# An attention and MLP kernel on one core: a tile's softmax kept in its scores' PSUM bank, the low half of g in the next slot, global results turned on TensorE

## The chip, the cores and the metric

One core of a Trainium2 chip. The metric is device microseconds (us) of one execution, lower is better. The profile is one execution, taken by the hardware profiler. Engines: PE is TensorE's matmul and PEld its weight load, DVE is VectorE, ACT is ScalarE, POOL is GpSimd, and SP is the engine whose queue issues the DMAs here. SBUF is the working memory, PSUM the banks into which PE writes.

## The reference

Eight batches with eight heads of attention over 512 local and 32 global positions, then a two-layer product over all 4608 tokens. A local query sees the 32 global keys and the local keys within 32 positions; a global query sees all keys.

```python
k_all = np.concatenate([k_g, k_l], axis=2); v_all = np.concatenate([v_g, v_l], axis=2)
out_g = np.matmul(sm(scale * np.matmul(q_g, k_all.transpose(0, 1, 3, 2))), v_all)
s_ll = np.where(np.abs(pos[:, None] - pos[None, :]) <= 32, scale * np.matmul(q_l, k_l.transpose(0, 1, 3, 2)), -1e9)
out_l = np.matmul(sm(np.concatenate([s_lg, s_ll], axis=-1)), np.concatenate([v_g, v_l], axis=2))
x = np.concatenate([out_g, out_l], axis=2).transpose(0, 2, 1, 3).reshape(4608, 512)
h = np.maximum(x @ w_in, 0.0)          # 512 -> 2048
return h * h @ w_out                   # 2048 -> 512
```

`sm` subtracts the row's maximum, takes the exponential and divides by the sum plus 1e-9.

## The kernel before, in words

**Tiles.** An attention tile t is one head of one half sequence: 256 queries (two groups u of 128), each group against 224 keys, out of 128 tiles. The first 16 tiles ("plain") are computed in float32, all others with operands split into a high and a low float32r half (`hi`/`lo`, `ph`/`pl`, `gh`/`gl`, `x_h`/`x_l`, `ws`): three products in place of one. The MLP runs in 17 blocks of 256 tokens, of eight steps m each; a step forms 256 of the 2048 hidden columns (`gemm1`, tile h), squares the positive part (`act1`), splits it (`act2`) and adds its share of the output (`gemm2`, tiles o).

**The slot.** One turn of the main loop holds tile t and step m = t - 9. The instructions of each engine are issued in the order in which the code names them (`InOrder`, from t = 17 on), so the code's order is each engine's queue. Within a slot, for tile t: `scores` (PE, tile s), `softmax1` (DVE: mask, scale, row minimum), `softmax2` (ACT: exponential with sums), `softmax3` (DVE: 1e-9 added to the sums, tile st, reciprocal, normalisation into prob), `turn` (POOL copies prob's 16-bit words into planes, then a transposing DMA into turned). For tile t - 1: `join` (POOL, turned to joined), `parts` (ACT, ph) and `parts_rest` (DVE, ph, ml, pl), and late in the slot `av` (PE, tile xa). For t - 2: `x_evac` (ACT x_h, DVE x_l). For t + 1: `split_qk` (ACT) and `split_qk_rest` (DVE), tile qk, from raw. For t + 2: `load_head`, the DMA of raw, into one of two buffers. `split_v` makes the two halves of tile t's v out of raw (ACT, DVE).

**PE's order** in a slot is h (24 matmuls), gs, half of o, now and then a global product gxo, the other half of o, xa of tile t - 1, s of tile t + 1. The scores of a tile lie in one PSUM bank (pool `ps_a`, tag "s"), which the next tile's scores take again.

**Global jobs.** Each group of four heads with its 32 global queries needs some fifteen jobs (`g_load_v`, `g_soft`, `g_turn`, `g_join`, `g_parts`, `g_av`, `g_x` and so on). The dictionary `jobs` sets each at a slot, relative to d, and at a place in the slot. Two such groups fall into 16 slots. `g_av` writes its result gxo into the bank of xa, ACT scales it into xs, and `g_x` turns it by four DVE transposes of 32x32 into xg.

**Shared ports.** DVE and POOL both work on SBUF: POOL's copies are joined, planes, and for the global jobs gp<-sg (`g_turn`) and sg<-gq (`g_join`).

Of the kernel before, what the change touches and what calls it, by code (L numbers as in the profile page):

```python
# [17 lines left out]
P = 128  # L18
# [41 lines left out]
def attention_moe(  # L60
# [88 lines left out]
    def split_v(t):  # L149
        raw = heads[t]["raw"]  # L150
        v = heads[t]["v"] = p2.tile([P, 2, 192], F32R, tag="v", name=f"v{t}")
        ac.copy(v[:, 0, :], raw[:, QK:])
        ve.tensor_sub(v[:, 1, :], raw[:, QK:], f(v[:, 0, :]))

    def scores(t):
        hd = heads[t]
        pool, tag = (ps_h, "h") if t < 8 and t % 2 else (ps_a, "s")
        s = pool.tile([P, 2, WIN], F32, tag=tag, name=f"s{t}")
# [12 lines left out]

    def softmax1(t):
        hd = heads[t]
        hf = (t // 8) % 2
        pr = p2.tile([P, QK + QC], F32, tag="qk", name=f"pr{t}")[:, : 2 * WIN] if plain(t) else prob
        hd["pr"] = pr
        st = p2.tile([P, 8], F32, tag="st", name=f"st{t}")
        for u in range(2):
            m = 2 * hf + u
            ve.tensor_tensor_reduce(  # L180
                out=pr[:, WIN * u : WIN * (u + 1)],
                in0=hd["s"][:, u, :],
                in1=masks[:, WIN * m : WIN * (m + 1)],
                scale=-scale(t),
                scalar=3.0e38,
                op0=ALU.add,
                op1=ALU.min,
                accum_out=st[:, u : u + 1],
            )
        hd["st"] = st  # L190

    def softmax2(t):
        st = heads[t]["st"]
        pr = heads[t]["pr"]
        for u in range(2):
            w_ = pr[:, WIN * u : WIN * (u + 1)]
            ac.activation(
                out=w_, in_=w_, func=AF.Exp, scale=-1.0, bias=st[:, u : u + 1], accum_out=st[:, 4 + u : 5 + u]
            )

    def softmax3(t):
# [41 lines left out]
    def parts_rest(t):  # L243
# [4 lines left out]
        ve.tensor_sub(pl.rearrange("p (c n) -> p c n", c=2), sides(joined), sides(f(ph)))  # L248

    def av(t):  # L250
        hd = heads[t]
        c = QC + KC
        if plain(t):

            xa = ps_a.tile([P, HALF], F32, tag="xa", name=f"xa{t}")
            v, pts = hd["raw"][:, c:], hd["pts"]
# [5 lines left out]
        else:  # L262
            xa = ps_a.tile([64, HALF], F32, tag="xa", name=f"xa{t}")
            v, ph, pl = hd["v"], hd["ph"], hd["pl"]
# [13 lines left out]
    def x_evac(t):  # L278
# [123 lines left out]
    def g_av(t, pair):  # L402
        (gvh, gvl), (pth, ptl) = state["gvs"], state["gpt"]
        xo = ps_a.tile([64, P], F32, tag="xa", name=f"gxo{t}_{pair}")
        mm = []
# [4 lines left out]
        for i, (x, y) in enumerate(mm):  # L410
            pe.matmul(xo, x, y, start=i == 0, stop=i == len(mm) - 1)
        xs = p1.tile([64, P], F32, tag="xs", name=f"gxs{t}_{pair}")
        ac.activation(out=xs, in_=xo, func=AF.Copy, scale=state["gst", t][:64, pair : pair + 1])
        state["xs"] = xs

    def g_x(t, pair):
        b, grp, xs = t // 16, (t // 4) % 2, state["xs"]
        for j in range(2):
            h = 4 * grp + 2 * pair + j
            for dd in range(2):  # L420
                r = (h % 2) * 64 + 32 * dd
# [73 lines left out]
    def act2(m):  # L495
# [118 lines left out]
    for t in range(NSTEP + LAG + 1):  # L614
# [40 lines left out]
        for place in (4, 3):
            for job, *args in jobs.pop((t, place), ()):
                job(*args)
        if done:
            evac(m // 8 - 1, (1,))
# [154 lines left out]
```

## Time and profile before

| | |
|---|---|
| median of three runs | 1070.45 us (1070.18 to 1073.39) |
| the profiled execution | 1071.19 us, of which the span of the program's instructions 1069.1 |
| busy: PE, PEld | 1029.5 (96%), 902.3 (84%) |
| busy: DVE, ACT, POOL | 867.7 (81%), 721.5 (67%), 385.0 (36%) |
| chain that ended last | PE 43%, DVE 37%, ACT 8%, issue 5%, DMA 3%, POOL 2% |
| granted PE clock, mean | 0.994 |

The span falls into a start in float32 that is bound by loads and PE (to about 106 us), five slots in which the last weights are split (to 154 us), the steady part (to 961 us) and an end in which only the MLP is left. Matmuls are pipelined, so PE's busy time is a union of overlapping intervals. A row of a group of instructions ends in its busy time, the mean of one in ns, and the engine's idle time just before them; a row by tile gives minimum/median/maximum in ns. DVE instructions that are held up show as long instructions, not as idle time.

### The profile page before, as it was taken

To read this page: it belongs to the slowest core of one execution; us is meant where nothing else is said; L and a number is where in the kernel's file an instruction comes from. 1 tells how busy PE (TensorE), PEld (TensorE's weight loads), DVE (VectorE), ACT (ScalarE), POOL (GpSimd) and SP (SyncE) were. 2 spreads that over 40 slices of the span, in tenths; PEclk is the share of its full clock that TensorE was granted. 3 is DMA by queue.
4 is the path that set the end of the run, shared out by engine and by line. 5 is a ranking of instruction groups with operands and counts; after the bars stand their busy time and mean duration, and the time that the engine had idled before them with its cause. 6 is when DMAs were issued, how large, how long until landed. Compare 5 with 4: busy or idle time off the path is not lost.

```text
span 1069.1 us, 20564 instructions
## 1 busy us (share of the span) xinstructions
PE 1029.5 (96%) x7040; PEld 902.3 (84%) x7040; DVE 867.7 (81%) x2445; ACT 721.5 (67%) x1743; POOL 385.0 (36%) x544
## 2 busy tenths in 40 slices
PE   8999989999999999999999999999999999999998
PEld 6776778988898888888888889888888888889896
DVE  5689878899989888898979999898989999893311
ACT  6889766767767766767666766776667676664432
POOL 1010344444445343444444443453445353441000
PEclk9999989999999999999999999999999999999999
DMA  9772444445444544454544444545444454341000
GB/s 367 310 258 80 104 103 115 114 116 125 116 123 101 136 103 101 115 118 123 122 115 116 116 120 109 123 104 125 125 110 105 118 135 110 103 95 54 5 21 20
DMA packets 193576, 127.69 MB, mean 119 GB/s; under 512 B 143552, under 2 KB 168640, under 8 KB 193472
## 3 DMA queue, kind: packets, MB, share of 16 engines
q1 hardware_dynamic: 193328, 126.32, 44.5%
q8 instruction: 55, 0.90, 0.4%
q14 instruction: 49, 0.40, 0.1%
q10 hardware_dynamic: 144, 0.07, 0.0%
HBM read 82.84 MB, written 8.91 MB: 86 GB/s over the span
## 4 chain that ended last, share of the span: by engine, by line
PE 43%; DVE 37%; ACT 8%; issue 5%; DMA 3%; POOL 2%; SPq 0%; DVEq 0%; POOLq 0%; ACTq 0%
PE o L53 17%; PE h L53 16%; DVE prob L53 6%; DVE st L53 5%; DVE qk L53 5%; PE xa L53 4%; ACT prob L53 3%; DVE v L53 3%; PE s L53 3%; DVE gl L53 2%; PE gxo L53 2%; DVE x_l L53 2%; DVE ph L53 2%; DVE pl L53 2%; DMA raw<-in_pk_dram 2%
## 5 line engine op out<-in xcount | busy, mean ns | idle before, releaser
L53 PE MATMUL h<-x_h,ws 128*128 128x256 f32 x2048 | 391.4, 284 | 0.0
L53 PEld LDWEIGHTS h<-x_h,ws 128*128 128x128 f32 x2048 | 329.1, 192 | 0.7
L53 PE MATMUL o<-ws,gh 128*128 128x512 f32 x1024 | 324.4, 398 | 3.2 <-ACT ot L53 3.0
L53 PE MATMUL h<-x_l,ws 128*128 128x256 f32 x1024 | 290.9, 284 | 1.1 <-DVE x_l L53 1.1
L53 POOL COPY joined<-turned 128x1024 uint16<-128x1024 uint16 x112 | 155.3, 1387 | 378.1 <-DMA turned<-planes 232.9
L53 POOL COPY planes<-prob 128x448 uint16<-128x448 uint16 x336 | 171.3, 547 | 152.1 <-DVE prob L53 152.1
L53 PEld LDWEIGHTS o<-ws,gh 128*128 128x128 f32 x1024 | 182.5, 189 | 38.2 <-ACT ot L53 7.0
L53 PE MATMUL o<-ws,gl 128*128 128x512 f32 x512 | 202.1, 395 | 0.0
L53 PEld LDWEIGHTS h<-x_l,ws 128*128 128x128 f32 x1024 | 197.0, 192 | 3.2 <-DVE x_l L53 2.6
L53 ACT ACTIVATE prob<-prob,st 128x224 f32<-128x224 f32 x224 | 106.3, 475 | 90.3 <-DVE st L53 89.5
L53 DVE TENSOR_TENSOR gl<-pt,gh 128x512 fp32r<-128x512 f32 x128 | 87.5, 684 | 73.2 <-ACT gh L53 72.0
L53 DVE TENSOR_TENSOR qk<-raw,qk 64x352 fp32r<-64x352 f32 x224 | 109.1, 487 | 8.7 <-ACT qk L53 1.6
L53 PEld LDWEIGHTS o<-ws,gl 128*128 128x128 f32 x512 | 96.3, 188 | 23.1
L53 ACT ACTIVATE pt<-h 128x512 f32<-128x512 f32 x128 | 74.2, 580 | 54.3 <-PE h L53 54.0
L53 ACT CAST x_h<-xa 64x256 fp32r<-64x256 f32 x120 | 43.7, 364 | 98.2 <-PE xa L53 97.9
L53 ACT CAST ph<-joined 128x512 fp32r<-128x512 f32 x112 | 68.9, 615 | 41.2 <-POOL joined L53 39.0
L53 PE MATMUL s<-qk 128*128 128x224 f32 x448 | 83.5, 298 | 8.2 <-DVE qk L53 5.6
L53 DVE TENSOR_SCALAR st<-st 128x2 f32<-128x2 f32 x128 | 62.5, 488 | 34.0 <-ACT prob L53 29.8
L53 ACT CAST qk<-raw 128x608 fp32r<-128x608 f32 x112 | 78.1, 697 | 8.7 <-DMA raw<-in_pk_dram 8.6
L53 DVE TENSOR_TENSOR v<-raw,v 128x192 fp32r<-128x192 f32 x112 | 80.5, 719 | 0.0
L53 DVE CUSTOM_DVE_ANT_0 prob<-s,con 128x224 f32<-128x224 f32 x224 | 77.7, 382 | 3.0 <-PE s L53 1.3
L53 ACT ACTIVATE pt<-pt 128x512 f32<-128x512 f32 x128 | 74.5, 582 | 4.0
(85 smaller groups left out, 1616.9 us busy)
## 6 DMA issues: line engine op xcount, KB each, us to landing
raw<-in_pk_dram SPq DMA_DIRECT2D x112, 400.0 KB, 3.5
wr<-in_w_dram SPq DMA_DIRECT2D x32, 512.0 KB, 8.0
gv<-in_vg_dram SPq DMA_DIRECT2D x32, 320.0 KB, 3.8
out_dram<-ot SPq DMA_DIRECT2D x32, 256.0 KB, 2.4
raw<-in_pk_dram SPq DMA_DIRECT2D x15, 432.0 KB, 8.2
qr<-in_qg_dram SPq DMA_DIRECT2D x31, 64.0 KB, 3.1
turned<-planes SPq DMA_TRANSPOSE x112, 3.1
out_dram<-ot SPq DMA_DIRECT2D x8, 64.0 KB, 1.7
```

Source lines behind the costliest of these rows:

```text
L53: r = method(*args, **kwargs)
```

## The change

For tiles from 16 on, `softmax1` writes its masked scores back into the scores' bank and `softmax2` takes the exponential in place there; the normalisation reads the bank and writes prob to SBUF. The sums go into two columns of the PSUM tile of xa (that of tile t - 2, read out by then), and st reads them there. The low half gl of step m - 1 is computed in slot m (`act2_rest`), behind `softmax1`. `split_qk`, its rest, `parts` and its rest follow the normalisation, in this order, and the low half of v comes last (up to tile 21 it stays early). Both output evictions stand ahead of the exponential, and their tiles take the buffers of gl and gh instead of two of the global jobs'. The global jobs are at other slots and places; gxo lies in the scores' bank, and the turning of the result is one PE transpose into 64 free columns of that bank and two ACT copies, in place of four DVE transposes.

```diff
+    def work(t, u):
+        hd = heads[t]
+        return hd["pr"][:, WIN * u : WIN * (u + 1)] if plain(t) else hd["s"][:, u, :]
     def softmax1(t):
...
-                out=pr[:, WIN * u : WIN * (u + 1)],
+                out=work(t, u),
     def softmax2(t):
+        su = st[:, 4:6] if plain(t) else state["xa"][:, HALF:]
...
-                out=w_, in_=w_, func=AF.Exp, scale=-1.0, bias=st[:, u : u + 1], accum_out=st[:, 4 + u : 5 + u]
+                out=w_, in_=w_, func=AF.Exp, scale=-1.0, bias=st[:, u : u + 1], accum_out=su[:, u : u + 1]
     def softmax3(t):
-        ve.tensor_scalar(out=st[:, 6:8], in0=st[:, 4:6], scalar1=1e-9, scalar2=None, op0=ALU.add)
+        ve.tensor_scalar(out=st[:, 6:8], in0=heads[t]["sums"], scalar1=1e-9, scalar2=None, op0=ALU.add)
...
-                ve.tensor_scalar(out=w_, in0=w_, scalar1=st[:, 2 + u : 3 + u], scalar2=None, op0=ALU.mult)
+                ve.tensor_scalar(out=to, in0=work(t, u), scalar1=by, scalar2=None, op0=ALU.mult)
+    def out_bank(t):
+        state["xa"] = ps_a.tile([P, HALF + 2], F32, tag="xa", name=f"xa{t}")
+        return state["xa"]
     def g_av(t, pair):
-        xo = ps_a.tile([64, P], F32, tag="xa", name=f"gxo{t}_{pair}")
+        xo = ps_a.tile([P, 512], F32, tag="s", name=f"gxo{t}_{pair}")[:64, :P]
     def g_x(t, pair):
-                ve.transpose(
+        xt = state["s"][:, 2 * WIN :]
+        pe.transpose(xt, state["xs"], ident[:64, :64])
+    def g_x_copy(t, pair):
+            ac.copy(xg[r, 2 * grp + pair, 32 * b : 32 * b + 32], xt[r, 32 * j : 32 * j + 32])
     def act2(m):
-        ve.tensor_sub(gl, r, f(gh))
+    def act2_rest(m):
+        ve.tensor_sub(gl, moe["r"], f(gh))
     def evac(blk, tiles=(0, 1)):
-            pool, tag = ((p1, "ptl"), (p1, "gvl"))[i]
+            pool, tag = ((p2, "gl"), (p2, "gh"))[i]
```

In the main loop the calls of a slot are put in another order (a job's second number is its place in the slot):

```diff
         if live:
             softmax1(t)
+        if 8 < m <= NSTEP:
+            act2_rest(m - 1)
...
         if live and not early:
             split_v(t)
+            if t < LATE:
+                split_v_rest(t)
+        for job, *args in jobs.pop((t, 7), ()):
...
         if live:
             softmax2(t)
-        if new:
-            parts(t - 1)
+        for job, *args in jobs.pop((t, 4), ()):
...
         if live and not early:
             softmax3(t)
             turn(t)
+        for job, *args in jobs.pop((t, 9), ()):
...
+        if t + 1 < NT and not early:
+            split_qk(t + 1)
+        if new:
+            parts(t - 1)
+        if not early:
+            if t + 1 < NT:
+                split_qk_rest(t + 1)
+            if new:
+                parts_rest(t - 1)
+            if live and t >= LATE:
+                split_v_rest(t)
         if NPLAIN <= t + 2 < NT:
             load_head(t + 2)
```

And the jobs of a global group, each with its slot and place:

```diff
+            first = t % 8 == 3
+            k = d + 7 if first else d + 6
-                (d + 4, 3, g_parts),
-                (d + 4, 0, g_av, 0),
-                (max(d + 5, 17), 3, g_x, 0),
-                (d + 5, 2, g_split_v, 1),
-                (max(d + 6, 17), 0, g_av, 1),
-                (max(d + 7, 18), 3, g_x, 1),
+                ((d + 5, 9, g_parts) if first else (d + 4, 3, g_parts)),
+                (d + 5, 0, g_av, 0),
+                (d + 5, 0, g_xs, 0),
+                (d + 6, 7, g_x, 0),
+                (d + 6, 4, g_x_copy, 0),
+                ((d + 6, 3, g_split_v, 1) if first else (d + 5, 1, g_split_v, 1)),
+                (k, 0, g_av, 1),
+                (k, 0, g_xs, 1),
+                (k + 1, 7, g_x, 1),
+                (k + 1, 4, g_x_copy, 1),
```

DVE's queue in slot 78, before the change, from the second masked reduction on (the number behind a tile's name is the attention tile or the step: gl69 belongs to step 69):

```order
L53 TENSOR_TENSOR v78_7375<-raw78_7191,v78_7375 128x192
L53 TENSOR_SCALAR st78_7359<-st78_7359 128x2
L53 RECIPROCAL st78_7359<-st78_7359 128x2
L53 TENSOR_SCALAR prob_93<-prob_93,st78_7359 128x224 x2
L53 TENSOR_TENSOR gvl75_0_7393<-gv75_0_7124,gvh75_0_7392 128x512
L53 TENSOR_TENSOR gvh75_0_7392<-gv75_0_7124,gvh75_0_7392 32x128
L53 TENSOR_TENSOR ph77_7380<-joined_96,ph77_7380 32x256
L53 TENSOR_TENSOR ml_97<-joined_96,ph77_7380 64x128
L53 TENSOR_TENSOR pl77_7415<-joined_96,ph77_7380 128x256
L53 TENSOR_TENSOR qk79_7411<-raw79_7286,qk79_7411 64x352
L53 TENSOR_TENSOR qk79_7411<-raw79_7286,qk79_7411 128x256
L53 TENSOR_TENSOR gl69_7446<-pt_100,gh69_7445 128x512
```

The same slot of the changed kernel:

```order
L54 TENSOR_TENSOR gl68_7325<-pt_100,gh68_7324 128x512
L54 TENSOR_SCALAR st78_7342<-xa76_7314 128x2
L54 RECIPROCAL st78_7342<-st78_7342 128x2
L54 TENSOR_SCALAR prob_93<-s78_7335,st78_7342 128x224 x2
L54 TENSOR_TENSOR qk79_7371<-raw79_7278,qk79_7371 64x352
L54 TENSOR_TENSOR qk79_7371<-raw79_7278,qk79_7371 128x256
L54 TENSOR_TENSOR ph77_7373<-joined_96,ph77_7373 32x256
L54 TENSOR_TENSOR ml_97<-joined_96,ph77_7373 64x128
L54 TENSOR_TENSOR pl77_7377<-joined_96,ph77_7373 128x256
L54 TENSOR_TENSOR v78_7359<-raw78_7183,v78_7359 128x192
L54 TENSOR_TENSOR gvl75_0_7385<-gv75_0_7108,gvh75_0_7384 128x512
L54 TENSOR_TENSOR gvh75_0_7384<-gv75_0_7108,gvh75_0_7384 32x128
```

The low half of step 68 has come in from the slot before, v has gone from the front to behind pl, the qk pair stands ahead of ph, and the global job's pair (gvl, gvh) has moved from the middle to the end.

ACT's queue in slot 81, before, from the high half of v on:

```order
L53 CAST v81_7693<-raw81_7489 128x192
L53 ACTIVATE prob_93,st81_7677<-prob_93,st81_7677 128x224 x2
L53 CAST ph80_7698<-joined_96 128x512
L53 CAST qk82_7723<-raw82_7608 128x608
L53 ACTIVATE pt_100<-h72_7680 128x512
```

And of the changed kernel, where a transposed global result falls into this slot:

```order
L54 CAST v81_7668<-raw81_7481 128x192
L54 ACTIVATE s81_7644,xa79_7630<-s81_7644,st81_7651 128x224 x2
L54 COPY xg_90<-s81_7644 64x32 x2
L54 CAST qk82_7683<-raw82_7584 128x608
L54 CAST ph80_7685<-joined_96 128x512
L54 ACTIVATE pt_100<-h72_7655 128x512
```

The exponential now works on s81 in PSUM and puts its sums into xa79, the two copies of the turned result stand behind it, and the cast of qk comes ahead of that of ph.

More of the change, by code (lines that the diff above doesn't have):

```diff
@@ L36 @@
 WCH = 32
+LATE = 22
 def f(ap):
@@ L81, in attention_moe @@
     heads = {}
+    state = {"s": None}
     def plain(t):
@@ L152, in split_v, with split_v_rest @@
         ac.copy(v[:, 0, :], raw[:, QK:])
+    def split_v_rest(t):
+        raw, v = heads[t]["raw"], heads[t]["v"]
         ve.tensor_sub(v[:, 1, :], raw[:, QK:], f(v[:, 0, :]))
@@ L157, in scores @@
         pool, tag = (ps_h, "h") if t < 8 and t % 2 else (ps_a, "s")
-        s = pool.tile([P, 2, WIN], F32, tag=tag, name=f"s{t}")
+        s = pool.tile([P, 512], F32, tag=tag, name=f"s{t}")
+        state["s"] = s
+        s = s[:, : 2 * WIN].rearrange("p (u n) -> p u n", u=2)
         for u in range(2):
@@ L253, in av @@
         if plain(t):
-            xa = ps_a.tile([P, HALF], F32, tag="xa", name=f"xa{t}")
+            xa = out_bank(t)[:, :HALF]
             v, pts = hd["raw"][:, c:], hd["pts"]
@@ L262, in av @@
         else:
-            xa = ps_a.tile([64, HALF], F32, tag="xa", name=f"xa{t}")
+            xa = out_bank(t)[:64, :HALF]
             v, ph, pl = hd["v"], hd["ph"], hd["pl"]
@@ L411, in g_av, with g_xs @@
             pe.matmul(xo, x, y, start=i == 0, stop=i == len(mm) - 1)
+        state["xo"] = xo
+    def g_xs(t, pair):
+        xo = state["xo"]
         xs = p1.tile([64, P], F32, tag="xs", name=f"gxs{t}_{pair}")
@@ L416, in g_x @@
     def g_x(t, pair):
-        b, grp, xs = t // 16, (t // 4) % 2, state["xs"]
-        for j in range(2):
-            h = 4 * grp + 2 * pair + j
-            for dd in range(2):
-                r = (h % 2) * 64 + 32 * dd
-                ve.transpose(
-                    out=xg[r : r + 32, h // 2, 32 * b : 32 * b + 32],
-                    in_=xs[32 * j : 32 * j + 32, 64 * j + 32 * dd : 64 * j + 32 * dd + 32],
-                )
+        if state["s"] is None:
+            state["s"] = ps_a.tile([P, 512], F32, tag="s", name=f"xt{t}_{pair}")
+        xt = state["s"][:, 2 * WIN :]
+        pe.transpose(xt, state["xs"], ident[:64, :64])
+        state["xt"] = xt
+    def g_x_copy(t, pair):
+        b, grp, xt = t // 16, (t // 4) % 2, state["xt"]
+        for j in range(2):
+            r = slice(64 * j, 64 * j + 64)
+            ac.copy(xg[r, 2 * grp + pair, 32 * b : 32 * b + 32], xt[r, 32 * j : 32 * j + 32])
     wraw, wf, whi, wlo = {}, {}, {}, {}
@@ L638, in attention_moe @@
         if done:
-            evac(m // 8 - 1, (0,))
+            evac(m // 8 - 1)
         if live:
             softmax1(t)
+        if 8 < m <= NSTEP:
+            act2_rest(m - 1)
         if run:
@@ L645, in attention_moe @@
             split_v(t)
+            if t < LATE:
+                split_v_rest(t)
+        for job, *args in jobs.pop((t, 7), ()):
+            job(*args)
         if live:
             softmax2(t)
-        if new:
-            parts(t - 1)
+        for job, *args in jobs.pop((t, 4), ()):
+            job(*args)
         if live and not early:
@@ L652, in attention_moe @@
             turn(t)
+        for job, *args in jobs.pop((t, 9), ()):
+            job(*args)
+        if t + 1 < NT and not early:
[9 more added lines that the diff above has]
+                split_v_rest(t)
         if NPLAIN <= t + 2 < NT:
             load_head(t + 2)
[L655 to L659, printed above, removed]
+        for job, *args in jobs.pop((t, 3), ()):
+            job(*args)
         w_tick(t, 0)
+        if t >= NT:
+            state["s"] = None
         if live and early:
@@ L670, in attention_moe @@
             scores(t + 1)
-        if t + 1 < NT and not early:
-            split_qk(t + 1)
         if run:
```

16 lines of the change are left out of this document (6 added, 10 removed).

## The prediction

> **What bounds the kernel now.** I read the page first, then the chain of work and the windows (busy time by stretch), and last the timeline of single slots. A slot is one turn of the main loop, from its first matmul into h to the next slot's; in the steady part it holds one attention tile t and one step m = t - 9 of the two big products. T0 is a slot's first h matmul.
>
> ```profile
> span 1069.1 us, 20564 instructions
> 275.40 2.88 PE h L53 x24
> ...
> 282.35 2.88 PE h L53 x24
> ...
> 286.75 0.78 PE gxo L53 x13
> ...
> 290.11 2.88 PE h L53 x24
> ```
>
> The last four rows are the chain between 270 and 300 us, start and length. Where TensorE (PE) is never kept waiting, a slot takes 282.35 - 275.40 = **6.95 us**, and one that also holds a global product (gxo) 290.11 - 282.35 = **7.76 us**, 0.81 more.
>
> ```profile
> 153.62:961.12 807.50, 323.94 (x2544) 1.00 0.47 115
> 153.62:961.12 807.50, 28.07 (x338) 1.00 0.47 115
> ```
>
> These are windows of PE on tile h and on tile gxo over the steady part: 2544/24 = 106 slots and 338/13 = 26 global products in 807.5 us. Unhindered they take 106 x 6.95 + 26 x 0.81 = 757.8. So **49.7 us** of waiting is all that a change off PE can win here. The windows of eight slots, t = 78 to 85, show where it sits (length, then PE, weight loads, DVE, ACT, POOL):
>
> ```profile
> 578.17:586.33 8.16, 7.80 (x53) 6.59 (x51) 7.86 (x19) 5.58 (x14) 4.71 (x8) 1.00 0.50 122
> 586.33:595.32 8.99, 8.18 (x66) 7.12 (x64) 8.64 (x22) 5.90 (x16) 4.74 (x5) 1.00 0.50 121
> 595.32:602.27 6.95, 6.95 (x53) 6.34 (x51) 6.35 (x22) 4.95 (x13) 2.56 (x4) 1.00 0.39 100
> 602.27:610.47 8.20, 8.00 (x65) 7.18 (x64) 6.65 (x20) 5.16 (x15) 3.12 (x4) 1.00 0.47 124
> 610.47:617.88 7.41, 7.33 (x53) 6.50 (x51) 7.02 (x22) 6.67 (x17) 2.55 (x4) 1.00 0.65 173
> 617.88:624.82 6.94, 6.94 (x53) 6.36 (x51) 6.03 (x22) 4.79 (x13) 2.75 (x4) 1.00 0.36 90
> 624.82:632.85 8.03, 7.66 (x53) 6.52 (x51) 7.82 (x19) 5.58 (x14) 4.71 (x8) 1.00 0.52 129
> 632.85:641.86 9.01, 8.17 (x65) 7.11 (x64) 8.72 (x20) 5.57 (x14) 4.75 (x5) 1.00 0.49 117
> ```
>
> Rows 2, 4 and 8 hold a gxo (66, 65 and 65 recorded matmuls against 53). Their excess over the floor is 1.21, 1.23, 0, 0.44, 0.46, 0, 1.08, 1.25: two heavy pairs (78/79, 84/85) carry 4.8 of 5.7 us, and in these DVE is busy for over 95% of the slot. **DVE's chain inside a slot ends last**, and it is long because DVE is held up:
>
> ```profile
> L53 DVE TENSOR_TENSOR v<-raw,v 128x192 fp32r<-128x192 f32 x106 | 76.9, 725 | 0.0
> L53 DVE TENSOR_SCALAR st<-st 128x2 f32<-128x2 f32 x106 | 58.9, 555 | 27.5 <-ACT prob L53 27.2
> L53 DVE TENSOR_TENSOR v<-raw,v x112: 343/522/1731, 58.4 to 953.8; 128x192 fp32r<-128x192 f32 x112
> L53 DVE TENSOR_SCALAR st<-st x128: 150/169/1621, 8.9 to 954.9; 128x2 f32<-128x2 f32 x128
> L53 DVE TENSOR_TENSOR x_l<-xa,x_h x120: 403/417/419, 39.6 to 968.1; 64x256 fp32r<-64x256 f32 x120
> L53 DVE TENSOR_TENSOR gl<-pt,gh x128: 670/683/693, 114.0 to 1060.1; 128x512 fp32r<-128x512 f32 x128
> ```
>
> The same instruction (v: 343 to 1731 ns; st, two numbers a row: 150 to 1621) stretches when a POOL copy runs beside it, as the next fence shows; x_l and gl, which read one operand from PSUM (xa, pt), never do (403 to 419, 670 to 693). Over the minimum, v and st lose 0.38 + 0.41 = **0.79 us a slot**.
>
> ```profile
> 579.24 1.20 DVE L53 TENSOR_TENSOR v<-raw,v 128x192 fp32r<-128x192 f32 x1
> 580.36 1.05 DVE L53 TENSOR_SCALAR st<-st 128x2 f32<-128x2 f32 x1
> ...
> 581.65 0.65 DVE L53 TENSOR_SCALAR prob<-prob,st 128x224 f32<-128x224 f32 x2
> ...
> 583.67 0.51 DVE L53 TENSOR_TENSOR ph<-joined,ph 32x256 fp32r<-32x256 f32 x1
> ...
> 584.42 0.41 DVE L53 TENSOR_TENSOR pl<-joined,ph 128x256 fp32r<-128x256 f32 x1
> 584.86 0.98 DVE L53 TENSOR_TENSOR qk<-raw,qk 64x352 fp32r<-64x352 f32 x2
> 578.93 1.36 POOL L53 COPY joined<-turned 128x1024 uint16<-128x1024 uint16 x1 [3.21 <-DMA turned<-planes]
> 580.20 1.73 POOL L53 COPY gp<-sg 128x1088 uint16<-128x1088 uint16 x4
> 582.19 1.71 POOL L53 COPY planes<-prob 128x448 uint16<-128x448 uint16 x3 [0.26 <-DVE prob L53]
> ...
> 588.39 1.76 POOL L53 COPY sg<-gq 128x1280 uint16<-128x1280 uint16 x1
> 579.89 0.18 ACT L53 ACTIVATION_READ_ACCUMULATOR prob<-prob,st 128x1 f32 x1
> 583.93 1.23 SPq L53 DMA_TRANSPOSE turned<-planes  x1
> 585.25 0.53 SPq L53 DMA_DIRECT2D raw<-in_pk_dram  x1
> ```
>
> Slot 78 on DVE, POOL, ACT (the last row of exp) and SP: v ends with joined, st ends only when gp's big copy has. pl is done at T0 + 6.66, qk at T0 + 7.67, while PE without waits would want pl at T0 + 6.25 and qk at T0 + 6.45 (floor slot: xa 0.66 and s 0.49 before the next h).
>
> **The change part by part.**
>
> *Softmax in PSUM, gl and v moved.* st then reads its sums from PSUM and the normalisation reads the scores' bank, as x_l and gl do now, so neither should be held up by joined or gp. v leaves the place beside joined. In slot 78 exp ends at 579.89 + 0.18 = 580.07, where st could start; gl (0.68) now fills DVE's wait for it. From there st 0.15, the reciprocal's 0.24 (581.41 to 581.65) and a normalisation of 0.65 + 0.1 (below) end near 581.2, against 582.3: **1.1 us earlier**. Then come the qk pair (0.98), ph, ml, pl (1.16, from 583.67 to 584.83) and 0.4 to 0.8 of waiting beside gp and planes: done near T0 + 5.6 to 6.0, inside 6.25. Since the longer chain of a slot with a transposed result (below) comes right before 84, I leave 0.1 to 0.2 of the 1.21 in 78, likewise in 84.
>
> *Price of the normalisation.* No row reads 128x224 alone from PSUM. x_l (256 columns, 415 ns) and gl (512, 683) give a line of 1.05 ns a column, hence 0.38 for 224, against 0.33 now (half of the pair's 0.65): +0.1 a slot on DVE, covered by the 0.79. Ends: 0 and 2 x (0.683 - 0.33) = 0.7 a slot.
>
> The Trainium skill, "VectorE: DVE Perf Modes", section "Why PSUM operands drop a tier", speaks against this part: an fp32 operand in PSUM loses the doubled rate. By that page's cycle table an estimate is 177 ns from SBUF and 358 from PSUM, 0.18 more each; the measured 330 already stands near the slower figure. By the page the sum would be 0.36 a slot worse on DVE, and about 1056 in all.
>
> *New waits.* The scores' bank is now free after the normalisation (T0 + 3.05) and no longer after the masked reduction (T0 + 1.1, where v starts). On PE's queue two things wait for it: s of the next tile, with all of the next h behind it (due near T0 + 6.45), and gxo, which moves into that bank (T0 + 4.4, 286.75 - 282.35): slack 3.4 and 1.3 us. In the four slots in sixteen with a transposed result, exp waits for one PE transpose in the middle of h (T0 + 1.45), and the normalisation for two ACT copies of 64x32 as well: that chain is some 0.8 us longer, and ends near T0 + 3.85, with pl at 6.4; up to 0.15 of stall each.
>
> *v late.* v reads raw, so raw's buffer is released at about T0 + 5.7 and no longer at T0 + 2; but SP issues that load behind the transposing DMA anyhow (585.25, behind 583.93 + 1.23). In a slot like 78, but without gp, the normalisation ends at T0 + 3.05 (581.2), planes at 4.6, the transposing DMA is issued by 5.85 and the load near T0 + 5.9.
>
> ```profile
> raw<-in_pk_dram SPq DMA_DIRECT2D x112, 400.0 KB, 3.5
> L53 ACT CAST qk<-raw x112: 691/697/717, 87.6 to 947.7; 128x608 fp32r<-128x608 f32 x112
> 522.85 1.19 POOL L53 COPY planes<-prob 128x448 uint16<-128x448 uint16 x3 [0.94 <-DVE prob L53]
> 66.31 0.60 PE L53 MATMUL pt<-con,pr 128*128 128x128 f32 x4
> L53 DVE STREAM_TRANSPOSE xg<-gxs 32x32 f32<-32x32 f32 x104 | 20.8, 200 | 1.1
> L53 ACT COPY sg<-gs 64x96 f32<-64x96 f32 x32 | 7.5, 235 | 0.0
> ```
>
> It lands 3.5 us later (first row), at T0 + 9.4, which is 2.45 us into the next slot, when ACT has finished exp. What hangs on it then needs 0.7 (ACT's cast, second row), 0.98, 1.16 and 0.4 to 0.5 of waiting beside planes (which took 1.71 beside DVE work and, third row, 1.19 without): pl at 5.8, inside 6.25. The margin is only 0.5 us.
>
> *Global jobs.* Off DVE go 104 transposes of 200 ns in the steady part, 20.8 us. Onto PE come 32 transposes of 64 columns: four of 128 columns took 0.60 together, 0.15 each, so I take 0.10, **+3.2 us** (ends 0 and 32 x 0.15 = 4.8). ACT gains 64 copies of at most 0.235, 15 us, hidden where ACT idles (4.95 us busy of 6.95 in slot 80). Both evictions of o now stand ahead of exp, one more than before, in two slots of sixteen; I leave 0.2 of stall for each.
>
> *What stays.* Slot 79 is set by POOL, not by DVE: gp's copies end at 581.93 as before, so planes (0.26 of waiting for prob goes), the transposing DMA, joined and then sg<-gq come only some 0.3 us earlier, the last near 588.1 to 589.85. raw (issued near 584.95) lands near 588.45, ACT's cast ends at 589.15, and DVE's qk pair, two SBUF operands, waits for sg<-gq to end at 589.85. pl is then done at 592.5. The slot would start at 585.25 and want it at 591.5: **1.0 us of the 1.23 stays**, and the same in 85.
>
> *Before and after the steady part* I cost nothing: in slots 17 to 21 the qk pair ahead of ph lengthens a chain that waits for raw, and one global product leaves slot 17; 3 us either way.
>
> **Sum.** Of the 5.67 us of excess in these eight slots some 2.3 to 2.5 stay (0.15 + 1.0 + 0.15 + 1.0 and crumbs), 42%; I take the same share of all 49.7, so 20.9 stay and 28.8 go. With +3.2 for PE: -25.6, and from the profiled execution's 1071.19 (its span and 2.1 around it) I come to **1046**. The median of the runs, 1070.45, is 0.7 lower, inside the rounding of this sum.
>
> **Rivals.**
> *PE runs at its floor* (1026): if raw lands a little sooner and sg<-gq does not hold qk, all 49.7 go, less 3.2, and 1071.2 - 46.5 = 1025. For it: slots 80 and 83 already stand at 6.95. Against: POOL's row of 588.39.
>
> *The waiting only moves* (1063): the qk pair now stands right behind the normalisation, where planes run, and reads two SBUF operands as v does. If it loses what v loses now (0.38) and the normalisation costs its upper end (0.7), DVE gains nothing but the 20.8 us of transposes, and about 40 of the 49.7 stay: 1071.2 - 9.7 + 3.2 = 1065, or 1063 with st's lock gone.
>
> [...]
>
> *Slower: raw late in every slot* (1085). v and the order qk before ph put everything behind raw's landing, with 0.5 us to spare. At a mean landing of 4.5 us instead of 3.5 each slot stalls 0.5, 53 us in 106 slots, and eats the gain of 46.5; at 4.6 to 4.7 it is 1085. It decides from 4.4 us on. For it: SP's queue and the 16 DMA engines also carry gv and the results; against it: the median of 112 loads is 3.5.
>
> *The change doesn't bite*: if reading PSUM does not free st, or a stall passes to gxo behind the scores' bank, the time stays within 3 us of now.
>
> **How the numbers follow.** Forecast (1036 to 1058) 0.55; floor 0.15; waiting moves (1058 to 1067) 0.13; no bite 0.08; raw late 0.09. About 0.3%, 3.2 us, is what a measurement can tell from no change. Faster by more: 0.55 + 0.15 + 0.13 = 0.83; within: 0.08; slower: 0.09. The range 1028 to 1068 leaves out the slow case, most of the no-bite case and the lowest part of the floor case, under 0.2.
>
> **What would show it.** Right: st at 0.15 to 0.2 us in every slot; v near 0.34; normalisation rows near 0.38; slots 78 and 84 near 7.1, slots 79 and 85 still about 1 us over their floor; PE busy up by 3 us, DVE down by some 80. Wrong: ACT's qk cast waiting for raw in most slots (raw late), the qk pair at 0.8 us or more (waiting moved), gxo waiting for the normalisation, or no slot above its floor (PE bound).

## The result, and the profile after

The changed kernel takes **1114.94 us** (median of four runs, 1112.13 to 1120.58) against 1070.32 in the same comparison: ratio 1.0417, interval 1.0367 to 1.0468. It is slower by 44.6 us, where 1046 was forecast with a range up to 1068. The profiled execution is the longest of the four, 1120.58. Of the executions behind the experiments below one, of e5, took 3494.32 us; its ratio is formed from the nine others (1069.05 to 1084.19, median 1075.60 where 1076.50 is given for all ten).

From the page of the changed kernel: span, busy times, and the chain that ended last.

```profile
span 1118.8 us, 20573 instructions
...
PE 1055.5 (94%) x7072; PEld 917.1 (82%) x7072; DVE 806.1 (72%) x2317; ACT 731.3 (65%) x1807; POOL 405.5 (36%) x544
...
PE 39%; DVE 26%; ACT 14%; DMA 12%; issue 5%; POOL 2%; SPq 0%; DVEq 0%; ACTq 0%; POOLq 0%
```

DVE did become lighter, 867.7 to 806.1 us, and its share of the chain fell from 37% to 26%. ACT's rose from 8% to 14% and DMA's from 3% to 12%: more of the chain runs through these two. The windows of the changed kernel on the slots 77 to 85 (length, then PE, weight loads, DVE, ACT, POOL, granted clock):

```profile
601.94:610.44 8.50, 7.71 (x53) 6.38 (x51) 6.22 (x21) 6.06 (x17) 3.04 (x4) 1.00 0.34 79
...
610.44:617.63 7.19, 7.17 (x52) 6.38 (x51) 6.36 (x19) 5.10 (x13) 5.62 (x8) 1.00 0.53 129
617.63:627.63 10.00, 8.24 (x53) 6.88 (x51) 7.47 (x22) 5.64 (x16) 5.08 (x6) 0.95 0.45 110
627.63:636.41 8.78, 8.78 (x64) 8.14 (x64) 6.29 (x18) 5.03 (x12) 3.68 (x5) 0.87 0.51 120
636.41:643.82 7.41, 7.40 (x53) 6.55 (x52) 6.00 (x17) 5.66 (x15) 2.43 (x4) 1.00 0.16 51
643.82:651.70 7.88, 7.88 (x66) 7.05 (x64) 6.92 (x21) 5.81 (x16) 3.04 (x4) 1.00 0.74 205
651.70:660.23 8.53, 7.40 (x54) 6.54 (x52) 5.90 (x20) 6.73 (x19) 3.01 (x4) 1.00 0.30 72
660.23:667.69 7.46, 7.40 (x52) 6.44 (x51) 6.61 (x19) 5.11 (x13) 4.75 (x8) 1.00 0.52 130
667.69:675.62 7.93, 7.54 (x53) 6.47 (x51) 7.01 (x19) 4.43 (x11) 4.70 (x5) 1.00 0.49 128
```

Slot 78 is 7.19 us, nearly as forecast (7.1), and 84 is 7.46. But 77, which stood at 6.94 before, is 8.50; 83, 6.94 before, is 8.53; 79 grew from 8.99 to 10.00; and 80 runs at a granted clock of 0.87. The rows with x64 and x66 hold a gxo: those of 79 and 81 have moved to 80 and 82. So slot 79 is now 3.05 us over its floor of 6.95, where it was 1.23 over 7.76. The steady part (slots 22 to 127) grew from 807.5 to 847.8 us, the slots 17 to 21 from 47.9 to 53.7, and what follows slot 127 from 108.0 to 111.1.

Groups of DVE instructions in the changed kernel, by shape, with minimum/median/maximum in ns:

```profile
L54 DVE TENSOR_TENSOR v<-raw,v x100: 340/343/347, 155.0 to 954.6; 128x192 fp32r<-128x192 f32 x100
L54 DVE TENSOR_SCALAR st<-xa x101: 158/159/164, 155.6 to 958.1; 128x2 f32<-128x2 f32 x101
L54 DVE TENSOR_SCALAR prob<-s,st x202: 439/449/454, 156.1 to 959.0; 128x224 f32<-128x224 f32 x101
```

In this stretch v and st are not held up any more. The normalisation, from PSUM, takes 0.45 us each.

**Where 0.7 us of a slot went.** Slot 78 before the change, DVE and ACT, from x_l to the end of the second exponential, and then the same of the changed kernel:

```profile
578.28 0.42 DVE L53 TENSOR_TENSOR x_l<-xa,x_h 64x256 fp32r<-64x256 f32 x1
...
578.92 0.38 DVE L53 CUSTOM_DVE_ANT_0 prob<-s,con 128x224 f32<-128x224 f32 x1
579.24 0.07 DVE L53 DVE_READ_ACCUMULATOR2_ANT st<- 128x1 f32 x1
...
579.03 0.48 ACT L53 ACTIVATE prob<-prob,st 128x224 f32<-128x224 f32 x1 [0.54 <-DVE st L53]
```

```profile
610.86 0.40 DVE L54 TENSOR_TENSOR x_l<-xa,x_h 64x256 fp32r<-64x256 f32 x1
...
611.49 0.13 DVE L54 DVE_READ_ACCUMULATOR2_ANT st<- 128x1 f32 x1
611.66 0.40 DVE L54 CUSTOM_DVE_ANT_0 s<-s,con 128x224 f32<-128x224 f32 x1
611.97 0.14 DVE L54 DVE_READ_ACCUMULATOR2_ANT st<- 128x1 f32 x1
...
613.19 0.16 DVE L54 TENSOR_SCALAR st<-xa 128x2 f32<-128x2 f32 x1 [0.53 <-ACT s L54]
...
613.66 0.81 DVE L54 TENSOR_SCALAR prob<-s,st 128x224 f32<-128x224 f32 x2
...
612.15 0.42 ACT L54 ACTIVATE s<-s,st 128x224 f32<-128x224 f32 x1 [1.38 <-DVE st L54]
```

Before, the first exponential ran beside the second masked reduction: it started at 579.03, the reduction at 578.92. Now it starts at 612.15, after that reduction's read-out (611.97 + 0.14). From x_l's start that is 1.29 us instead of 0.75; x_l itself starts 0.42 us into the slot, where it started at 0.11. The normalisation ends at 614.47, 4.03 us into the slot, where the prediction had near 3.0.

### The profile page after: what moved, and what is told of

It is laid out like the page before. It is cut to its first block, busy times and chain, and to the rows that moved or that the text cites. A ratio compares the mean times of both kernels' runs of the same rounds, so it can differ in the third digit from the quotient of the medians.

```text
span 1118.8 us, 20573 instructions
## 1 busy us (share of the span) xinstructions
PE 1055.5 (94%) x7072; PEld 917.1 (82%) x7072; DVE 806.1 (72%) x2317; ACT 731.3 (65%) x1807; POOL 405.5 (36%) x544
## 4 chain that ended last, share of the span: by engine, by line
PE 39%; DVE 26%; ACT 14%; DMA 12%; issue 5%; POOL 2%; SPq 0%; DVEq 0%; ACTq 0%; POOLq 0%
PE h L54 16%; PE o L54 14%; DMA raw<-in_pk_dram 11%; DVE qk L54 5%; DVE s L54 4%; PE xa L54 4%; ACT s L54 3%; PE s L54 3%; DVE ph L54 3%; ACT qk L54 2%; DVE st L54 2%; DVE prob L54 2%; DVE pl L54 2%; DVE x_l L54 2%; DVE ml L54 2%
## 5 line engine op out<-in xcount | busy, mean ns | idle before, releaser
L54 PE MATMUL h<-x_h,ws 128*128 128x256 f32 x2048 | 406.6, 289 | 0.0
L54 PEld LDWEIGHTS h<-x_h,ws 128*128 128x128 f32 x2048 | 337.5, 196 | 2.8
L54 POOL COPY planes<-prob 128x448 uint16<-128x448 uint16 x336 | 195.0, 617 | 170.1 <-DVE prob L54 170.1
L54 ACT ACTIVATE s<-s,st 128x224 f32<-128x224 f32 x224 | 95.0, 424 | 147.4 <-DVE st L54 96.4
L54 DVE TENSOR_TENSOR qk<-raw,qk 64x352 fp32r<-64x352 f32 x224 | 126.4, 564 | 41.8 <-ACT qk L54 37.8
L54 PE MATMUL xa<-ph,v 128*64 128x128 f32 (+1 forms) x672 | 80.2, 247 | 31.3 <-DVE ph L54 18.6
L54 PEld LDWEIGHTS xa<-ph,v 128*64 128x64 f32 x672 | 59.1, 135 | 55.3 <-DVE ph L54 23.2
L54 DVE TENSOR_SCALAR prob<-s,st 128x224 f32<-128x224 f32 x224 | 90.7, 446 | 13.4 <-POOL joined L54 0.5
L54 DVE CUSTOM_DVE_ANT_0 s<-s,con 128x224 f32<-128x224 f32 x224 | 88.4, 395 | 9.0 <-PE s L54 3.1
L54 DVE TENSOR_TENSOR x_l<-xa,x_h 64x256 fp32r<-64x256 f32 x120 | 49.7, 414 | 47.8 <-ACT x_h L54 47.0
```

The lines of the kernel that those rows point to most:

```text
L54: r = method(*args, **kwargs)
```

## The experiments

Each run also timed the kernel before on the same chip (1069.4 to 1071.0); times are medians.

**The place of the global maximum, from both sides.** In the changed kernel (e1) g_soft goes ahead of the qk pair; in the kernel before (e4) it goes to the slot's end.

```diff
-                (d + 1, 3, g_soft),
+                (d + 1, 9, g_soft),
```

> The changed kernel with g_soft (maximum of a global group, 0.85 us on DVE) at place 9, ahead of the qk pair, instead of behind everything. Theory A (the late maximum holds ACT's exp of sg, behind it x_h, then x_l): the slots t%16 = 13 and 3, now 8.50 and 8.53 us, fall to 6.95 to 7.2 and 7.4; x_l starts 0.6 us into slot 13 instead of 1.66; about 19 us go there and some 5 to 12 more in the slots 14/15 and 4/5 behind them, since joined starts earlier: 1082 to 1092. Theory B alone (only the late landing of raw matters): less than 5 us go, 1110 or more.

```diff
-                (d + 1, 3, g_soft),
+                (d + 1, 1, g_soft),
```

> The kernel before with one edit: g_soft behind gl, right ahead of the global exponential, as late as the change puts it. Theory A: ACT's exp of sg then waits about 0.9 us, x_h and x_l stand behind it, and the slots 13 and 3 grow from 6.95 by 1 to 1.5 us each: 1083 to 1092. If the place of the job is harmless: 1068 to 1073.

Measured: e1 **1095.83** (ratio 1.0242, 1.0208 to 1.0277), 19.1 under the changed kernel; e4 **1090.40** (1.0181, 1.0166 to 1.0197), 19.4 over the kernel before in its comparison (1071.0). The two sides agree. The mechanism in the changed kernel, around the start of slot 77 (601.94), DVE and ACT:

```profile
601.42 0.70 DVE L54 TENSOR_REDUCE gst<-sg 128x1 f32<-128x544 f32 x1
...
603.61 0.42 DVE L54 TENSOR_TENSOR x_l<-xa,x_h 64x256 fp32r<-64x256 f32 x1 [1.30 <-ACT x_h L54]
...
602.35 0.75 ACT L54 ACTIVATE sg<-sg,gst 128x544 f32<-128x544 f32 x1 [1.26 <-DVE gst L54]
...
603.22 0.37 ACT L54 CAST x_h<-xa 64x256 fp32r<-64x256 f32 x1
```

The maximum stands behind v at the end of slot 76. ACT's global exponential waits 1.26 us for it with x_h queued behind, and DVE then waits 1.30 us for x_h. In e1 slot 77 is 7.12 us (595.53 to 602.65). Theory A holds. e1 misses its range by 4 us, and no run shows by what; slots 79 and 85 of its trace are as long as before the edit (9.99 and 7.92 us).

**The order of qk and ph, and the load of raw.** e2 puts the cast of qk and the qk pair back behind ph, ml, pl.

```diff
-        if t + 1 < NT and not early:
-            split_qk(t + 1)
         if new:
             parts(t - 1)
         if not early:
-            if t + 1 < NT:
-                split_qk_rest(t + 1)
             if new:
                 parts_rest(t - 1)
...
+        if t + 1 < NT and not early:
+            split_qk(t + 1)
         if run:
             act1(m)
...
+        if t + 1 < NT:
             split_qk_rest(t + 1)
```

> The changed kernel with the cast of qk and the qk pair back behind ph, ml, pl, as before the change. Theory B (raw lands late, and ph and pl stand behind the qk cast on ACT and DVE): the slots 15 and 5, now 10.4 and 8.7 us in the mean, fall to 8.5 and 7.8, the clock stays at 1.00 in the slots 0 and 6 behind them, and 20 to 35 us go in all: 1080 to 1095. If the order does not matter, since raw holds s of the next tile anyway, 1108 to 1118. Slots 13 and 3 stay at 8.5 by theory A.

e3 splits v early and loads raw ahead of the transposing DMA:

```diff
-LATE = 22
+LATE = 999
...
             softmax3(t)
+        if NPLAIN <= t + 2 < NT:
+            load_head(t + 2)
+        if live and not early:
             turn(t)
...
-        if NPLAIN <= t + 2 < NT:
-            load_head(t + 2)
```

> The changed kernel with the low half of v early (between gl and st) in all slots and the load of raw ahead of the transposing DMA in SP's queue. Theory B: raw is issued some 3 us into the slot, lands before the next slot begins, ACT never waits for it; slots 15 and 5 lose 2.5 and 1 us, the clock dips behind them go: 1070 to 1085; v costs DVE up to 0.4 us a slot beside joined, where it mostly waits for the exponential. If the landing isn't what holds these slots: within 5 us of 1115.

Measured: e2 **1127.04** and e3 **1139.87**, both slower than the changed kernel. Theory B as I had put it falls: with raw issued first, ACT's cast of qk waits for it 8 times in the steady part (12.7 us) in place of 56 (56.8 us), and the kernel is slower all the same. In e2 the maximum comes ahead of the qk pair again, so slots like 77 shrink (8.49 to 7.08 in the mean), and still the whole is 12 us longer: beside e1 (steady part 830.4 us) the old order costs 28 us (858.8). Only the slots up to 21 gain: e2 reaches slot 22 at 154.0 us, the changed kernel at 159.9. Slots 84 and 85 of e2, POOL and ACT:

```profile
655.88 3.17 POOL L54 COPY gp<-sg 128x1088 uint16<-128x1088 uint16 x4
...
665.39 1.34 POOL L54 COPY joined<-turned 128x1024 uint16<-128x1024 uint16 x1 [4.60 <-DMA turned<-planes]
...
666.77 0.62 ACT L54 CAST ph<-joined 128x512 fp32r<-128x512 f32 x1 [3.51 <-POOL joined L54]
```

gp, which took 1.73 us before the change, takes 3.17 here. planes, turned and joined come late, and now ph waits. In e3 joined is late in raw's place: the transposing DMA is issued behind the load, and of 112 landings of turned 23 take over 4 us, where 13 did in the changed kernel. joined starts 5.5 us into slot 95, after a wait of 5.34 us for turned.

**Softmax in the bank, undone or alone.** In e5 (from e1) scores and exponential go back to SBUF, only the sums stay in PSUM. e6 does the first part of the change alone on the kernel before; e7 only the sums.

```diff
     def work(t, u):
         hd = heads[t]
-        return hd["pr"][:, WIN * u : WIN * (u + 1)] if plain(t) else hd["s"][:, u, :]
+        return hd["pr"][:, WIN * u : WIN * (u + 1)]
```

> As e1 (changed kernel, g_soft early), but the masked scores and the exponential go to prob in SBUF again; only the sums stay in PSUM. Theory P: in the changed kernel the first exponential starts only when the second masked reduction has been read out, since both work in the one bank (+1.71 us into the slot, where it was +0.86), so that the normalisation ends 0.8 us later in every slot, and with it planes, the transposing DMA, joined and the load of raw. Then here exp starts near +0.9, joined near +0.8 in place of +1.58, the slots 14/15 and 4/5 lose 0.5 to 1 us each, and the whole gets to 1070 to 1085. Theory Q (POOL's copies are stretched by DVE's work on SBUF, and exp's place is harmless): 1090 to 1100, with gp and planes as long as in e1 (1.9 to 2.9 us), or longer, as the normalisation reads SBUF again.

```diff
     def softmax1(t):
...
-                out=pr[:, WIN * u : WIN * (u + 1)],
+                out=work(t, u),
     def softmax2(t):
+        su = st[:, 4:6] if plain(t) else state["xa"][:, HALF:]
...
-            w_ = pr[:, WIN * u : WIN * (u + 1)]
+            w_ = work(t, u)
...
-                ... accum_out=st[:, 4 + u : 5 + u]
+                ... accum_out=su[:, u : u + 1]
     def softmax3(t):
...
-            w_ = pr[:, WIN * u : WIN * (u + 1)]
+            w_, to = work(t, u), pr[:, WIN * u : WIN * (u + 1)]
...
-                ve.tensor_scalar(out=w_, in0=w_, ...)
+                ve.tensor_scalar(out=to, in0=w_, ...)
```

> The kernel before with the first part of the change alone: masked scores, exponential and sums in PSUM, the normalisation from the bank. Theory P: st at 0.16 us in every slot (0.4 us less in the mean), but exp starts 0.8 us later; the plain slots, where qk stood at +5.97 and is wanted near +6.45, grow by some 0.1 to 0.4, the heavy ones shrink by 0.2 to 0.5: 1068 to 1085. If the later exponential costs nothing, as the forecast had it: 1045 to 1058.

```diff
-                ... accum_out=st[:, 4 + u : 5 + u]
+                ... accum_out=su[:, u : u + 1]
```

> The kernel before with only the sums in PSUM; reductions, exponential and normalisation as before in SBUF. exp starts as early as before (+0.86). If st's stretch alone is the loss: st 0.16 us and 1045 to 1058. If the instruction behind it (the normalisation, from SBUF to SBUF) is held by POOL's copy in its place: its longest goes from 1.46 us in few slots to over 1 us in most slots with gp or sg<-gq, and the time stays at 1065 to 1073.

Measured: e5 **1076.50** (1.0055, 1.0022 to 1.0088), 19.3 under e1. e6 **1105.76** (1.0325, 1.0298 to 1.0352): the part of the change from which the gain was to come costs 35 us by itself, where I expected 14 at most. e7 **1078.06** (1.0068, 1.0047 to 1.0089). Slot 77 of e6, where x_l starts as early as before:

```profile
589.55 0.42 DVE L53 TENSOR_TENSOR x_l<-xa,x_h 64x256 fp32r<-64x256 f32 x1
...
590.86 0.14 DVE L53 DVE_READ_ACCUMULATOR2_ANT st<- 128x1 f32 x1
...
592.54 0.81 DVE L53 TENSOR_SCALAR prob<-s,st 128x224 f32<-128x224 f32 x2
...
591.03 0.42 ACT L53 ACTIVATE s<-s,st 128x224 f32<-128x224 f32 x1 [1.91 <-DVE st L53]
```

Again the exponential starts behind the second read-out, and the normalisation ends 3.8 us after x_l's start. Over the slots 23 to 126 (104 of them, times from x_l's start in each trace, medians) the first exponential starts 0.82 us after x_l before the change, 1.48 in the changed kernel, 1.47 in e6, 0.88 in e5; the normalisation ends at 3.08, 3.80, 3.79 and 3.01. e7 misses its range on the upper side: st is free (0.16 us), the normalisation is held instead (0.48 us in the mean where it was 0.36), and the global copies it runs beside stretch (gp in slots like 78 from 1.73 to 2.30 us), so that slots like 79 grow from 8.97 to 10.83 in the mean while those like 78 shrink from 8.24 to 7.42.

**The wait alone.** Is it the exponential's wait, or reading PSUM? e15 (on the kernel before) and e16 (on e5) issue the second group's exponential first. Its data come from the second reduction, so the first exponential to run has the wait, and nothing moves to PSUM.

```diff
-        for u in range(2):
+        for u in range(2) if plain(t) else (1, 0):
             ...
             ac.activation(
```

> The kernel before with one edit: of a tile's two exponentials, the one on the second group is issued first, so that the first to run waits for the second masked reduction, as in the changed kernel. Nothing moves to PSUM. Theory P (that wait is what makes the softmax in one bank dear): the first exponential starts near +1.35 in slots like 77 in place of +1.02, the normalisation ends 0.15 to 0.35 us later, less where v is being stretched; 1074 to 1090. If the wait is harmless and the price lies in PSUM itself (longer reads and normalisation): 1069 to 1073.

> The same swap in e5 (changed kernel, g_soft early, only the sums in PSUM), where no v stands in front of st to cover it: 0.35 us later in every slot, nearly half of what e1 has against e5 (0.8 us, 19 us in all): 1080 to 1092. If the wait is harmless: 1073 to 1079.

Measured: e15 **1090.65** (1.0196, 1.0178 to 1.0215), 21 over the kernel before; e16 **1089.91** (1.0193, 1.0142 to 1.0245), 13.4 over e5. By the same medians the first exponential starts 1.19 us after x_l in both, 0.3 to 0.4 later than without the swap, and the normalisation ends about 0.3 later. That much delay, in every slot, costs 13 to 21 us; the bank's 0.7 to 0.8 costs 19 to 35. Theory P is shown by adding and by taking away. Much of the price is what the delay meets later: of e15's 20.6 us in the steady part 12 lie in the seven slots like 79 (8.97 to 10.69 us in the mean). There joined starts 3.73 us into slot 79, behind a late turned, and the slots 31, 79 and 111 run at a granted clock of 0.85, 0.76 and 0.85.

**The transposed results.** e8 (from e1) turns them by DVE again.

```diff
-        pe.transpose(xt, state["xs"], ident[:64, :64])
+                ve.transpose(out=xg[...], in_=xs[...])
...
-                (d + 6, 7, g_x, 0),
-                (d + 6, 4, g_x_copy, 0),
+                (d + 6, 3, g_x, 0),
```

> As e1, but the global results are turned by four DVE transposes, as before the change, at place 3; no transpose on PE, no copies on ACT, gxo still in the scores' bank. If a PE transpose in the middle of h costs 0.39 us (slots 8 and 1: h 3.27 us with it, 2.88 without) and delays exp and the normalisation behind it, 32 of them are 12 us and more: 1078 to 1086. If DVE's 0.8 us a result now ends last instead: 1092 to 1100.

Measured: **1093.21** (1.0204, 1.0162 to 1.0246), not apart from e1. Both theories are half right. Windows of the changed kernel on slots 88 and 89, with such a transpose and without:

```profile
692.50:699.84 7.34, 7.34 (x54) 6.53 (x52) 5.38 (x16) 4.94 (x14) 3.02 (x4) 1.00 0.31 81
699.84:706.78 6.94, 6.94 (x52) 6.36 (x51) 5.91 (x18) 5.01 (x15) 3.04 (x4) 1.00 0.41 95
```

It costs PE 0.40 us with no wait in it. But DVE's transposes cost as much in two busy slots: those like 82 grow from 8.10 to 8.97 us, those like 84 from 7.62 to 8.35.

**POOL's order.** If POOL's round (joined, gp, planes, DMA, joined) bounds the heavy slots, planes should go ahead of gp and of sg<-gq.

```diff
-                (d + 3, 6, g_turn),
-                (d + 4, 6, g_join),
+                (d + 3, 3, g_turn),
+                (d + 4, 3, g_join),
```

> As e5 (changed kernel, g_soft early, only the sums in PSUM), with POOL's global copies behind planes: gp<-sg after planes and after the load of raw on SP, sg<-gq after planes of the next slot, the split of the turned weights one slot later for one group. Theory R (the heavy slots are set by POOL and the DMA: joined, gp, planes, transposing DMA, joined again, some 9.3 us round, which freeing DVE can't shorten): planes starts right behind the normalisation (near +3.5 instead of +4.7), raw and turned land some 1.5 us earlier, the slots 15 and 5 fall from 9.1 to below 8 us: 1055 to 1066. If DVE's queue is what holds them: 1072 to 1080.

> The kernel before with POOL's global copies behind planes in the same way, and the global product one slot later (its second split of v at the slot's end). Theory R: joined in slots 15 and 5 stays near +0.8, ACT's cast of ph no longer waits, sg<-gq and what hangs on it leave the slot's chain; of some 34 us of excess in the slots 14, 15, 4, 5 half goes: 1045 to 1060. If the stretched DVE operations (v, st) set these slots, they meet planes and gp later in the slot instead: 1065 to 1075.

> As e10, with the sums in PSUM in addition. In e7 that cost 7 us, which theory R puts down to gp and planes being stretched by the DVE work that st had held back. With gp behind planes the freed st should be worth something: 1040 to 1058, 0 to 8 us under e10. If the sums in PSUM cost by themselves: 5 to 8 us above e10.

In these three the second global group's weights are overwritten by the next scores before they are split; all instructions run. Measured: e9 1061.00, e10 1054.39, e11 1054.76. e12 to e14 move that group's softmax, turning and joining one slot earlier (`e = d if first else d - 1`), and its weights are split in time.

> As e10, but the second global group of every sixteen slots does its softmax, turning and joining one slot earlier, so that its weights are split before the next scores come into sg. Theory R: as e10, 1050 to 1060, under 0.99 of the kernel before. If the gain of e10 came from the later split: 1062 to 1073.

> As e9 (changed kernel, g_soft early, only the sums in PSUM, POOL's global copies behind planes), with the second group's softmax, turning and joining one slot earlier. Theory R: as e9, 1053 to 1066. If not: 1072 to 1080, as e5.

> As e13, but with the softmax in the scores' bank, as the change has it. Theory P and R together: the exponential that waits for both reductions makes the normalisation, planes, turned and joined 0.8 us later in every slot, but with gp and sg<-gq behind planes the round through POOL and the DMA has that slack in most slots: between e13 and e13 + 8 us, 1055 to 1072. If the late exponential costs the same whatever POOL does: 19 us over e13, 1074 to 1084.

Measured: **e12 1056.39** (0.9865, 0.9847 to 0.9883), faster than both kernels. e13 1074.08 (1.0033, 1.0020 to 1.0045), e14 1108.73 (1.0365, 1.0340 to 1.0391). POOL and SP in slots 78 and 79 of e12:

```profile
576.88 1.71 POOL L53 COPY planes<-prob 128x448 uint16<-128x448 uint16 x3 [0.93 <-DVE prob L53]
578.54 2.87 POOL L53 COPY gp<-sg 128x1088 uint16<-128x1088 uint16 x4
581.83 1.36 POOL L53 COPY joined<-turned 128x1024 uint16<-128x1024 uint16 x1 [0.42 <-DMA turned<-planes]
...
578.62 1.24 SPq L53 DMA_TRANSPOSE turned<-planes  x1
579.95 0.54 SPq L53 DMA_DIRECT2D raw<-in_pk_dram  x1
```

gp may now take 2.87 us; nobody waits for it. planes no longer follows it, joined starts with slot 79 (581.79), and that slot takes 7.36 us. Its gxo has moved to slot 80, so over the floor slot 79 fell from 1.23 to 0.41 us and slot 80 rose from 0 to 0.36; over the whole steady part 807.5 us became 794.5. The order is not the only edit, though: in e9, e10 and e12 the weights of at least one of the two groups are also split a slot later, and how much of the gain is the order's was not separated. In e13, where each group's split stays in its slot, the reorder gives 2.4 us against e5, not clear of the noise, and e13 lies where its text put the failure of theory R. e11, 0.4 us from e10, shows that the sums in PSUM cost nothing once gp stands behind planes, and gain nothing either. The bank costs 34.7 us beside e13 (e14): my expectation that the late exponential would fit into POOL's slack was wrong. Why the earlier group costs e13 13 us over e9, but e12 only 2 over e10, stays open; e13 has it in slots like 84, 85 and 87 (7.28 to 7.97, 8.11 to 8.69 and 8.19 to 8.89 us in the mean).

## Why the prediction was wrong

- **The step that failed** is "In slot 78 exp ends at 579.89 + 0.18 = 580.07, where st could start". It took the exponential's time from the trace of before, though the change moves both reductions and both exponentials into one PSUM tile. There the first exponential starts only behind the second reduction's read-out. st itself fell as forecast (0.16 us), but in slot 78 it starts 2.75 us into the slot (613.19 - 610.44), where exp's old end, 580.07 - 578.17, would have let it at 1.90; of these 0.85 us 0.54 is the exponential's and 0.31 x_l's later start. I listed what waits for the bank on PE's queue and not what waits for it between DVE and ACT. The Trainium skill, "PSUM — Partial Sum Buffer", section "PSUM bank collisions raise a hardware error", has the rule: the compiler back end's scheduler adds a dependency between instructions of two engines that touch the same bank and quadrant, ACT and DVE too, and other addresses in that bank do not help. The trace agrees (612.15 against 611.97 + 0.14). It was the rule to weigh here; the one on the doubled rate bears on the price of one instruction.
- **The global jobs.** The prediction counted transposes, copies and evictions, and not that place 3 now lies behind v. That is 19 us (e1, e4), and nothing of it was in the sum.
- **What stays** was mis-sized: of the 49.7 us over the floor in the steady part 20.9 were to stay, and 90.0 did (847.8 - 757.8); 1.0 us was to stay in slot 79, and 3.05 did. The step had gp's copies end "as before", 3.76 us into slot 78 (581.93 - 578.17), and planes as long as before. But joined started 1.57 us into the slot in place of 0.76, gp ended at 4.76 (615.20), and planes, which took 1.71 us, took 2.91. So the load of raw behind it on SP was issued only 1.78 us into slot 79 (619.41 - 617.63), and ACT's cast waited. That a DVE which is no longer held lengthens POOL's copies is shown by e7, where only the sums moved and gp grew; for planes it is argued.

Slots 78 and 79 of the changed kernel, POOL, SP, ACT:

```profile
612.01 1.35 POOL L54 COPY joined<-turned 128x1024 uint16<-128x1024 uint16 x1 [3.21 <-DMA turned<-planes]
613.27 1.93 POOL L54 COPY gp<-sg 128x1088 uint16<-128x1088 uint16 x4
615.14 2.91 POOL L54 COPY planes<-prob 128x448 uint16<-128x448 uint16 x3
...
618.08 1.23 SPq L54 DMA_TRANSPOSE turned<-planes  x1
619.41 0.52 SPq L54 DMA_DIRECT2D raw<-in_pk_dram  x1
...
622.86 0.71 ACT L54 CAST qk<-raw 128x608 fp32r<-128x608 f32 x1 [2.15 <-DMA raw<-in_pk_dram]
```

raw's issue comes 8.97 us behind slot 78's start, where the prediction had 584.95 - 578.17 = 6.78. Of the rival "raw late in every slot" the sign came true in half of them: ACT's cast of qk waits for raw in 56 of the 106 slots of the steady part, 56.8 us together, where it waited in 4 for 2.6 us before. Its mechanism did not: the landing took 3.4 us in the median, under its point of 4.4. What was late is the issue, and not only behind a global copy: 7.41 us into the slot in the median of the slots 22 to 125, 6.56 before, where the prediction had 5.9 for a slot like 78 without gp. (Its sum for that rival, 1085 at 4.6 to 4.7 us, comes out at 1088 to 1099: 0.6 to 0.7 us in 106 slots on 1025.) Of the rival "the waiting only moves" less than half came: the qk pair takes 1.15 us in the mean (655 and 491 ns), 0.98 before, a loss of 0.17 in place of 0.38.

- **PE's transposes**: 0.10 us each was taken, 0.40 measured, 12.8 us for 32 in place of 3.2. PE's busy time rose by 26 us, in part at a lower clock: length times missing share of the clock, added up over the steady part's slots, is an estimated 15 us, 2 before.
- **Right**: st and v; DVE down, by 62 us of the 80 forecast. Slot 78 came out near 7.1 (7.19) with a later chain than forecast: pl was done 6.48 us into it (616.51 + 0.41), not at 5.6 to 6.0, and the 6.25 that PE asked for covered most of that. Slot 84 (7.46) did not come as near. The normalisation's price is 0.23 us a slot (two times 449 - 335 ns, medians), inside the range of 0 to 0.7 and over the 0.1 taken.
- **The head**, costed at nothing with 3 us either way, lost 5.7, by the order of qk and ph (e2).

The sum of what the runs undo one after another: late maximum 19.1, bank 19.3, and 5.6 to 6 left in e5 over the kernel before. Of the 69 us between forecast and result these two are 38; the rest is those 6 and the gain of 25 that did not come. In e5's profiled execution (1084.19, its longest fast one) the slots 17 to 21 take 52.0 us and what follows slot 127 takes 111.4, together 7.6 more than before, and the steady part 813.5, 6.0 more. What those consist of wasn't separated.

## What to carry to other kernels

Before moving a pipelined pair of steps into one PSUM bank, list which engines touch the bank and in what order: here two engines that overlapped on different halves of an SBUF tile ran one after the other in the bank. A stretched instruction in a profile can be one side of a shared resource; when it is freed, ask what it was holding back for others, and look at the copies and transfers on the other side. Where a copy engine's result starts a DMA round, try that copy first in its queue, ahead of copies that nobody waits for soon; together with a later split this gave 14 us on the kernel before.

## What was not expected of the hardware

In the changed kernel PE's clock falls in or after slots with much waiting, though the longest single wait of the one shown is 1.14 us. PE at the end of slot 79 of the changed kernel:

```profile
625.73 0.45 PE L54 MATMUL xa<-ph,v 128*64 128x256 f32 x2 [1.14 <-DVE ph L54]
...
626.69 1.14 PE L54 MATMUL s<-qk 128*128 128x224 f32 x4
```

The four matmuls into s take 1.14 us, where those at the end of slot 80 take 0.65, and slot 80 runs at 0.87 with PE busy throughout (8.78 of 8.78 us), 1.02 over its floor. Slot 79 was 3.05 us over its floor, with 1.14 the longest wait in it; behind slot 85, 0.98 over, the following window (675.62 to 684.25) shows 1.00. All 14 slots of the steady part with a granted clock under 0.99 are 10.0 us long or longer, or come right behind a slot of 9.84 or more; in e5 slots of 9.84 and 9.88 us pass without. The Trainium skill, "TensorE: Matmul & The Clock Gate", section "What's actually happening", has the gate close after an idle window of about 3.4 us; waits in several pieces sufficed here, and no run tells what share of such a window must be idle.

A masked reduction that writes PSUM starts 0.17 us after the first one's read-out began (611.49 to 611.66), where the SBUF form starts with it.
